# A thirteenth row buffer for three score-matrix pieces, half-block turns for all tiles, and a new order, in a fused spectral filter and expert lookup

## The chip, the cores and the metric

The kernel runs on one core of a Trainium2 chip. The metric is the device time of one execution in microseconds (us). The core has TensorE (PE in the profile, its weight loads PEld), VectorE (DVE), ScalarE (ACT), GpSimd (POOL), SyncE (SP) and 16 DMA engines. On-chip memory has 128 partitions; SBUF holds tiles, PSUM takes what TensorE writes.

## The reference

For `x` of 2048 tokens by 576 features the result is a gated sum of two branches.

```python
g = sigmoid((x * gate_w).sum(-1))
X = rfft2(x); a = irfft2(X * (w_r + 1j * w_i))          # branch A
q = einsum("nd,dhc->nhc", x, w_q)                        # branch B, 32 heads, 2 x 128 each
s1 = q[..., :128] @ k1.T;  s2 = q[..., 128:] @ k2.T      # 64 scores each
e  = argmax(s1) * 64 + argmax(s2)                        # one of 4096 experts a token and head
act = gelu(einsum("nd,nhd->nh", x, u[e]))
b = einsum("nh,nhd->nd", act, v[e])
out = g * a + (1 - g) * b
```

The softmax over one candidate is one in value. `u` and `v` are 4096 by 576 in float32, so a token needs 32 rows of `u` and 32 of `v`, which differ from token to token.

## The kernel before

**Tiles and chunks.** The tokens lie in 16 tiles of 128, the heads in 8 chunks of 4. Tiles 0 to 10 (`E_T`, "early") have their expert rows loaded while the scores are still being computed; tiles 11 to 15 (`L_SEQ`, "late") have theirs loaded in the second stage.

**First stage.** For each chunk the score weights and keys are multiplied into a score matrix in five pieces along the features. A piece is built by `build_m`: its weights are loaded by SyncE into a row buffer (`load_wq`, L428), TensorE multiplies them by the keys into half a PSUM buffer, ScalarE copies a rounded high piece to SBUF (`mh`, L526), TensorE subtracts that, and ScalarE copies the rest, the low piece (`ml`, L536). `MB` and `MBL` are the numbers of buffers for high and low pieces. `BUILD` says in which of the eight steps of a chunk each of the next chunk's pieces is built; two pieces of the same step share a PSUM buffer. A step (`scores`) multiplies two tiles of x, split in high and low parts as well, by the five pieces: 28 matmuls of 512 columns into one PSUM buffer. VectorE takes the maxima (L577), ScalarE marks them by signs (L584, L606), VectorE turns the marks into expert numbers (L608 to L626). `SOLO` counts first steps of chunk 0 that are read out one tile at a time.

**Row groups** (`group`). One group is a tile and a chunk: four gathers by GpSimd (L671), each bringing for 128 tokens the row of `u` and of `v` of one head, 4608 bytes a token, into one row buffer. The row buffers are the ring `uv` (`NG` of them), which the weight pieces share; the second stage has `NG2` more (`uv2`). VectorE multiplies the `u` rows by x and sums (L683), ScalarE applies the gelu (L689), VectorE multiplies in the factor (L698). Then there are two ways to sum the `v` rows, by the tile:

- way "v": VectorE adds each scaled row to the tile's sum (L711).
- way "t" (tiles in `T_T`): ScalarE scales each row into the other half of a neighbour's buffer (L724), and TensorE turns the scaled rows by an identity into PSUM, where they add up. For an early tile the PSUM sum of one group is added to the tile's sum by VectorE (L771); for a late one it grows over all chunks. `HALF` and `HALF_L` (early, late) choose between turns of 128x128 and two turns of 64x64 on half the partitions each (`turn`). `TJ` and `TJ_L` (early, late) say how many rows are scaled before a batch of turns is put out: a batch of two rows is one pair.

**Second stage.** It does the two-dimensional transform of branch A: fold the tiles (`fold`; tiles in `FOLD_V` are folded by VectorE first and need half as many matmuls), ten units of frequency work, the inverse per tile (`invert`; tiles in `INV_P` leave a sum and a difference to TensorE), the gates, the mix and the output. The late tiles' row groups run beside it in the order of `SEQ`, at which the last group of the late tile before the last is summed in way "v".

**The order.** All work is described as jobs with an engine, an estimated time, a due time and buffers. The class `Plan` simulates the engines with the ring sizes, always takes the ready job with the earliest due time whose buffers are free, and so writes one order for each engine. TensorE, VectorE, ScalarE, GpSimd and SyncE then run their lists strictly in that order, with waits where data or buffers are needed. Due times come from constants: `TP0` and `TPS` are the distance of score steps in chunk 0 and after it, `X0` and `X_GAP` place the loads of x, `LE` and `AHEAD` the row groups and their gathers, `TLAG` and `TGS` the late groups, `FPACE` the transform, the `AT_` constants single kinds of jobs. `LEAD`, `LEAST`, `LAND`, `ALONE`, `SHARE`, `DENSE` and `SLOWER` are the planner's model of gathers and of the TensorE clock.

Of the kernel before, what the change touches and what calls it, by code (L numbers as in the profile page):

```python
# [27 lines left out]
NCH = 8  # L28
# [60 lines left out]

LAG = {"DVE": 0.1, "ACT": 0.2, "PE": 0.0}  # L90
HOPS = {('PE', 'DVE'): 0.12, ('PE', 'ACT'): 0.46, ('PE', 'POOL'): 0.64, ('ACT', 'PE'): 0.28, ('ACT', 'DVE'): 0.02, ('ACT', 'POOL'): 0.01, ('DVE', 'POOL'): 0.4}
LEAD = 1.341
LEAST = -11.809
LAND = 4.039
ALONE = 0.716
SHARE = 0.426
WINDOW = 3.41
DENSE = -2.439
SLOWER = 1.649


class Plan:
# [37 lines left out]
    def order(self):  # L140
# [34 lines left out]
        def flow(t):  # L175
            nonlocal moved, turn
            both = bool(lines["POOL"] and lines["SP"])
            for e, q in lines.items():
                if q:
                    j = q[0]  # L180
                    rate = (1.0 if len(q) > 1 else ALONE) * (SHARE if both else 1.0) if e == "POOL" else (1.0 - SHARE if both else 1.0)
                    rest[j] = rest[j][0] - (t - moved) * rest[j][1], rate
# [9 lines left out]
        def clock(t, us, dense):  # L192
            nonlocal slow, window, seen
            x = t
            while True:
                k = int(x // WINDOW)
                if k != window:
                    slow = k > window + 1 or seen < DENSE * WINDOW
                    window, seen = k, 0.0
                edge = (k + 1) * WINDOW  # L200
                f = SLOWER if slow else 1.0
                if x + us * f <= edge:
# [15 lines left out]
        while events:  # L218
            t = events[0][0]
            while events and events[0][0] <= t:  # L220
# [8 lines left out]
                elif kind == "moved":  # L229
                    j, k = j  # L230
                    if k == turn:
                        flow(t)
                        lines[j.eng].popleft()
                        flow(t)
                        close(j, max(t, j.start + LEAST) + LAND if j.eng == "POOL" else t + 1.3)
                elif kind == "end":
# [10 lines left out]
            for eng, q in todo.items():  # L247
# [35 lines left out]
                if got.move:  # L283
                    push(t + (LEAD if eng == "POOL" else 1.9), "queue", got)
                else:
# [22 lines left out]
def tile_kernel(ctx, tc, xn, xT, wqT, wqL, kT, wri, uv, uw, gw, t_kr, t_fi, t_fe, t_tw, t_io, out):  # L308
# [32 lines left out]
    for tag, n in (("cand", CN), ("z", 8), ("b", 8), ("a", 8), ("im", 1), ("fe", 2), *((("dg", NDG),) if NDG else ()), ("mx", 2), ("sg", 2), ("sq", 1), ("ramp", 1), ("eq", EQN), ("sr", SRN)):  # L341
        ring(tag, "sm", n)
    ring("uv", "gp", NG)
    NY = len([t for t in T_T if t < NE])
# [115 lines left out]
    last = {}  # L460
# [200 lines left out]
    def group(t, c, at, ahead, gate_by=()):  # L661
# [49 lines left out]
                    dv(0.731, at, lambda v=v, s=s: stt(y.ap, v(), s(), y.ap, op0=ALU.mult, op1=ALU.add), [y], [(rows[k], 1), (a, k)])  # L711
            return
        part = t in E_T
        last = c == NCH - 1 - (TAILV if t == SEQ[-2][0] and t in T_T else 0)
        part_ = part and not paired(t, c)
        first = c == 0 or (part and not paired(t, c - 1))
        if first:
# [87 lines left out]
    order = sorted(((t, c) for c in range(NCH) for t in E_T), key=place)  # L805
    due = lambda n: when(n * 8 / NE + LE)
    todo = list(enumerate(order))
    for s in range(NCH * 8):
        c, tp = divmod(s, 8)
# [311 lines left out]

    TR = T0 + TLAG
    for n, t in enumerate(range(NT)):
# [44 lines left out]

NT2 = 5
SCRATCH = 2048  # L1170
NG = 12
NG2 = 3
LE = 3.125
NE = 11
MB = 8
MBL = 8
TPS = 7.047
AHEAD = -45.811
TLAG = 27.448
FPACE = 1.413  # L1180
BUILD = (3, 5, 6, 7, 7)
E_T = tuple(range(NE))
L_SEQ = tuple(range(NE, NT))
_PAIRS = ((14,), (13,), (12,), (11, 15))
SEQ = [(t, c) for p in _PAIRS for c in range(NCH) for t in p]
TGS = 8.225


LOW_PE = True
# [2 lines left out]
TRANS = 0.109  # L1192
TRANS2 = 0.062
SWITCH = 0.14
HALF = 0
HALF_L = 1
GX = 4
GT = 4
LOW_V = ()
LOW0 = 1  # L1200
LATE_G = 1
Z0 = 0.5
X0 = 9.48
TJ = 2
TJ_L = 4
BUILT = 0.1
ISSUE = 0.845
MOVE = 1.368
X_GAP = 4.311
GATE = -10.202  # L1210
HOLD_ML = 1.992
HOLD_A = 0.08
HOLD_T = 0.263
HOLD_D = 0.0
D_T = ()
T_T = (2, 3, 4, 6, 7, 10, 11, 12, 13, 14)
D_L = ()
FLIP = ()
AT_GELU = -46.223
AT_SCALE = 9.213  # L1220
AT_SUM = -94.03
AT_FOLD = -9.381
FOLD_V = (0, 1, 4, 5, 6, 8, 10, 11, 12, 13, 14)
GATE0 = 34.612
NA = 8
XL0 = -187.592
FI0 = -71.365
TURN = 1
MXO = 15.524
SGO = -56.575  # L1230
FILL = 0
FILLED = 8.11
TAILV = 1
TP0 = 12.235
X2 = 59.927
X4 = -0.154
XN0 = 11.008
INV_P = (0, 1, 2, 4, 8, 9, 10, 12, 14, 15)
SOLO = 0
SOLO_AT = -7.687  # L1240
SGO0 = 22.859
SOLO_P = 222.219
GL0 = 208.398
GL = 1.201
TWO = ()
CN = 3
EQN = 6
SRN = 4
ODD = (2, 7)


def paired(t, c):
    return t in TWO and c >= 0 and c + 1 < NCH and c % 2 == (t in ODD)


def how(t, c):
    if t == SEQ[-2][0] and c >= NCH - TAILV:
        return "v"
    if t in T_T:
        return "t"  # L1260
    return "d" if t in D_L or (t in D_T) != ((t, c) in FLIP) else "v"
# [49 lines left out]
```

## Time and profile before

| what | value |
|---|---|
| runs shown | 948.02, 948.95, 943.16 us, median 948.02 |
| profiled execution | 941.52 us, its span 939.7 us |
| instructions in the span | 18504 |
| moved by DMA | 344.16 MB, of them 302.02 MB by the gathers |
| row gathers | 512, first at 32.5 us, last at 918.5 us |

A group row of the profile reads: line, engine, operation, what it writes and reads, count, busy time, mean length of one in ns, idle time of the engine just before, and what ended that. A row of the order of time reads: start, length, engine, line, operation, tiles, shape, count, and in brackets the idle time before it with its releaser. A row of waits reads: who waited, for whom, us in total, times, longest. A row of a stretch reads: from and to, length, then busy time and instructions of each engine, the granted TensorE clock, the share of the DMA engines and the GB/s.

### The profile page before, as it was taken

The numbers are of one execution on the slowest core, as the hardware profiler recorded it, in microseconds if no ns is written. First come the engines' busy times: TensorE is split into PE (matmuls) and PEld (weight loads), VectorE is DVE, ScalarE is ACT, GpSimd is POOL, SyncE is SP. The second block draws the span as 40 slices with busy tenths as digits, with TensorE's granted clock in tenths as the row PEclk, the third lists the DMA queues.
The fourth block names the chain that finished last, engine by engine and source line by source line (L and its number), as shares of the span: only waits on it lengthen the run. The fifth ranks groups of instructions, "written<-read, shape, count | busy, mean of one in ns | idle before, by whom it ended". The sixth has DMA issues, their size and how long they took to land. (4 is left out here: it accounts for less than half of the span.)

```text
span 939.7 us, 18504 instructions
## 1 busy us (share of the span) xinstructions
PE 866.9 (92%) x6309; PEld 699.4 (74%) x6309; DVE 815.9 (87%) x2036; ACT 641.3 (68%) x2022; POOL 559.1 (59%) x516
## 2 busy tenths in 40 slices
PE   7899999999999998999999999967989999979993
PEld 6678887887877887888787777755767788756662
DVE  3578998998999999899999989898988898887888
ACT  3779888877877776876877777664646656654443
POOL 0416767756756656665665665667666556667560
PEclk9999999999999999999999999997999999999997
DMA  8968999999999999999999999899999999999993
GB/s 272 380 224 314 386 404 363 397 401 372 365 393 368 384 391 361 360 390 380 362 400 386 383 391 417 317 337 415 328 417 341 367 380 395 415 351 412 379 419 131
DMA packets 93218, 344.16 MB, mean 366 GB/s; under 512 B 10306, under 2 KB 14020, under 8 KB 93124
## 3 DMA queue, kind: packets, MB, share of 16 engines
q0 software_dynamic: 73728, 302.02, 83.7%
q1 hardware_dynamic: 19396, 40.96, 11.9%
q8 instruction: 50, 0.82, 0.3%
q14 instruction: 44, 0.36, 0.1%
HBM read 338.22 MB, written 4.72 MB: 365 GB/s over the span
## 5 line engine op out<-in xcount | busy, mean ns | idle before, releaser
L584 ACT ACTIVATE sg<-p,mx 128x64 bf16<-128x64 f32 x1024 | 227.1, 353 | 86.8 <-DVE mx L577 63.3
L671 POOL DMA_INDIRECT uv<-uv,eq x176 | 189.5, 1077 | 161.8 <-DVE xn L711 48.1
L683 DVE SCALAR_TENSOR_TENSOR uv<-uv,xn 128x576 f32<-128x576 f32 x352 | 259.9, 749 | 13.9 <-DMA uv<-uv,ei 4.6
L671 POOL DMA_INDIRECT uv<-uv,ei x178 | 199.9, 1123 | 104.8 <-issue 32.5
L724 ACT ACTIVATE uv<-uv,a 128x576 f32<-128x576 f32 x316 | 223.3, 784 | 19.7 <-DVE a L698 16.2
L372 PE MATMUL p<-ident,uv 64*128 64x64 f32 (+1 forms) x1980 | 159.7, 249 | 13.8 <-ACT uv L724 9.6
L372 PEld LDWEIGHTS p<-ident,uv 64*128 64x128 f32 (+1 forms) x1980 | 138.7, 140 | 41.3 <-ACT uv L724 16.7
L711 DVE SCALAR_TENSOR_TENSOR xn<-uv,a,xn 128x576 f32<-128x576 f32 x190 | 154.2, 812 | 0.5
L671 POOL DMA_INDIRECT uv<-uw,eq x80 | 88.2, 1103 | 52.5 <-issue 13.6
L683 DVE SCALAR_TENSOR_TENSOR uv<-uv,xl 128x576 f32<-128x576 f32 x160 | 116.0, 751 | 0.2
L372 PE MATMUL p<-mh,xha 128*128 128x512 f32 x256 | 106.3, 415 | 3.6 <-issue 2.4
L671 POOL DMA_INDIRECT uv<-uw,ei x78 | 81.2, 1042 | 41.0 <-issue 15.3
L372 PE MATMUL p<-mh,xh 128*128 128x512 f32 x256 | 103.5, 404 | 0.4 <-ACT sg L584 0.4
L372 PE MATMUL p<-ml,xha 128*128 128x512 f32 x256 | 101.1, 395 | 1.4 <-issue 1.4
L372 PE MATMUL p<-ml,xh 128*128 128x512 f32 x256 | 101.2, 395 | 0.6 <-issue 0.6
L372 PE MATMUL p<-mh,xoa 128*128 128x512 f32 x256 | 101.0, 395 | 0.5 <-issue 0.3
L372 PE MATMUL p<-mh,xo 128*128 128x512 f32 x256 | 101.1, 395 | 0.0
L372 PE MATMUL p<-fi,bt 128*128 128x289 f32 (+1 forms) x384 | 89.9, 429 | 1.1 <-ACT bt L917 0.7
L577 DVE TENSOR_REDUCE mx<-p 128x16 f32<-128x1024 f32 x64 | 77.9, 1218 | 13.9 <-PE p L372 11.8
L372 PEld LDWEIGHTS p<-fi,bt 128*128 128x128 f32 (+1 forms) x384 | 67.6, 242 | 19.1 <-issue 12.1
L606 ACT ACTIVATE sg<-sg 128x256 bf16<-128x256 bf16 x192 | 73.6, 424 | 0.8
L689 ACT ACTIVATE b<-z 128x4 f32<-128x4 f32 (+1 forms) x131 | 29.8, 228 | 62.7 <-DVE uv L683 52.1
(142 smaller groups left out, 1333.4 us busy)
## 6 DMA issues: line engine op xcount, KB each, us to landing
uv<-wqT SPq DMA_DIRECT2D x32, 512.0 KB
w<-wri SPq DMA_DIRECT2D x16, 289.0 KB
ml<-xT SPq DMA_DIRECT2D x16, 256.0 KB
xn<-xn SPq DMA_DIRECT2D x11, 288.0 KB
out<-xn SPq DMA_DIRECT2D x10, 288.0 KB
uv<-uv,ei POOLq DMA_INDIRECT x178
uv<-uv,eq POOLq DMA_INDIRECT x176
uv<-wqL SPq DMA_DIRECT2D x8, 256.0 KB
```

Source lines behind the costliest of these rows:

```text
L372: after("PE", nc.tensor.matmul(*args, **kw))
L577: dv(dve(1024), at - MXO, lambda: nc.vector.tensor_reduce(mv.ap[:, 2 * tp : 2 * tp + 2, :], ps.ap.rearrange("p a (g e) -> p a g e", e=E), ...
L584: on("ACT", actv(sg.ap[:, j, g, :], ps.ap[:, j, g * E : g * E + E], AF.Sign, bias=mv.ap[:, 2 * tp + j, g : g + 1], scale=-1.0))
L606: ac(0.307 if j is None else 0.2, at_, lambda b=b, s2=s2: actv(s2()[:, :, b * Q : b * Q + Q], s2()[:, :, b * Q : b * Q + Q], AF.Copy, bias ...
L671: on("POOL", nc.gpsimd.indirect_dma_start(out=g.ap.rearrange("p a d -> p (a d)"), out_offset=None, in_=table, in_offset=bass.IndirectOffse ...
L683: dv(0.677, at, lambda k=k, g=rows[k]: stt(g.ap[:, 0, :], g.ap[:, 0, :], 1.0, x.ap, op0=ALU.mult, op1=ALU.mult, accum_out=z.ap[:, k : k + 1]),
L689: ac(0.1, at + AT_GELU, lambda k0=k0, k1=k1: actv(b.ap[:, k0:k1], z.ap[:, k0:k1], AF.Gelu_apprx_tanh), [(b, k0)], [(z, k) for k in ks], ta ...
L711: dv(0.731, at, lambda v=v, s=s: stt(y.ap, v(), s(), y.ap, op0=ALU.mult, op1=ALU.add), [y], [(rows[k], 1), (a, k)])
L724: ac(0.667, at + AT_SCALE, lambda k=k, pair=pair, r=r: actv(pair.ap[:, r, :], rows[k].ap[:, 1, :], AF.Copy, scale=a.ap[:, k : k + 1]), [(p ...
```

## The change

The ring of row buffers has 13 in place of 12 in the first stage, and one fewer is added in the second, so that there are 15 as before. The high pieces have 7 buffers in place of 8, the low ones 6 in place of 8. Early tiles are turned in half blocks, as late ones are; their turns come in batches of four rows, those of the late tiles in batches of two. Tile 1 takes the place of tile 2 among those that are turned. Fewer tiles are folded by VectorE first (5, were 11), more are inverted without VectorE's sum and difference (12, were 10). Two steps of chunk 0 are read out one tile at a time. The late tiles come in the order 11, 12, 13, then 14 and 15 in turn. The due times and the planner's constants are new. The function `tail`, with `TAILW`, gives how many of a tile's last chunks are summed in way "v"; tile 15 is not in `T_T`, so that with these constants it is one chunk of tile 14, where it was one of tile 11.

```diff
--- before.py
+++ after.py
@@ -89,14 +89,14 @@
 
 LAG = {"DVE": 0.1, "ACT": 0.2, "PE": 0.0}
 HOPS = {('PE', 'DVE'): 0.12, ('PE', 'ACT'): 0.46, ('PE', 'POOL'): 0.64, ('ACT', 'PE'): 0.28, ('ACT', 'DVE'): 0.02, ('ACT', 'POOL'): 0.01, ('DVE', 'POOL'): 0.4}
-LEAD = 1.341
-LEAST = -11.809
-LAND = 4.039
-ALONE = 0.716
-SHARE = 0.426
+LEAD = 1.171
+LEAST = -32.411
+LAND = 3.551
+ALONE = 0.636
+SHARE = 0.3
 WINDOW = 3.41
-DENSE = -2.439
-SLOWER = 1.649
+DENSE = -3.314
+SLOWER = 1.108
 
 
 class Plan:
@@ -711,7 +711,7 @@
                     dv(0.731, at, lambda v=v, s=s: stt(y.ap, v(), s(), y.ap, op0=ALU.mult, op1=ALU.add), [y], [(rows[k], 1), (a, k)])
             return
         part = t in E_T
-        last = c == NCH - 1 - (TAILV if t == SEQ[-2][0] and t in T_T else 0)
+        last = c == NCH - 1 - tail(t)
         part_ = part and not paired(t, c)
         first = c == 0 or (part and not paired(t, c - 1))
         if first:
@@ -1168,22 +1168,22 @@
 
 NT2 = 5
 SCRATCH = 2048
-NG = 12
-NG2 = 3
-LE = 3.125
+NG = 13
+NG2 = 2
+LE = 2.716
 NE = 11
-MB = 8
-MBL = 8
-TPS = 7.047
-AHEAD = -45.811
-TLAG = 27.448
-FPACE = 1.413
-BUILD = (3, 5, 6, 7, 7)
+MB = 7
+MBL = 6
+TPS = 7.168
+AHEAD = -4.994
+TLAG = 93.11
+FPACE = 2.205
+BUILD = (2, 5, 5, 6, 6)
 E_T = tuple(range(NE))
 L_SEQ = tuple(range(NE, NT))
-_PAIRS = ((14,), (13,), (12,), (11, 15))
+_PAIRS = ((11,), (12,), (13,), (14, 15))
 SEQ = [(t, c) for p in _PAIRS for c in range(NCH) for t in p]
-TGS = 8.225
+TGS = 6.424
 
 
 LOW_PE = True
@@ -1192,69 +1192,76 @@
 TRANS = 0.109
 TRANS2 = 0.062
 SWITCH = 0.14
-HALF = 0
+HALF = 1
 HALF_L = 1
+TAILW = 1
 GX = 4
 GT = 4
 LOW_V = ()
 LOW0 = 1
 LATE_G = 1
 Z0 = 0.5
-X0 = 9.48
-TJ = 2
-TJ_L = 4
+X0 = 11.332
+TJ = 4
+TJ_L = 2
 BUILT = 0.1
-ISSUE = 0.845
-MOVE = 1.368
-X_GAP = 4.311
-GATE = -10.202
-HOLD_ML = 1.992
-HOLD_A = 0.08
-HOLD_T = 0.263
+ISSUE = 0.658
+MOVE = 1.325
+X_GAP = 5.028
+GATE = 5.201
+HOLD_ML = 1.359
+HOLD_A = 0.372
+HOLD_T = 0
 HOLD_D = 0.0
 D_T = ()
-T_T = (2, 3, 4, 6, 7, 10, 11, 12, 13, 14)
+T_T = (1, 3, 4, 6, 7, 10, 11, 12, 13, 14)
 D_L = ()
 FLIP = ()
-AT_GELU = -46.223
-AT_SCALE = 9.213
-AT_SUM = -94.03
-AT_FOLD = -9.381
-FOLD_V = (0, 1, 4, 5, 6, 8, 10, 11, 12, 13, 14)
-GATE0 = 34.612
+AT_GELU = 7.361
+AT_SCALE = 35.318
+AT_SUM = -22.122
+AT_FOLD = 6.917
+FOLD_V = (3, 4, 5, 13, 14)
+GATE0 = -38.732
 NA = 8
-XL0 = -187.592
-FI0 = -71.365
+XL0 = -138.691
+FI0 = 23.463
 TURN = 1
-MXO = 15.524
-SGO = -56.575
+MXO = 17.776
+SGO = -61.118
 FILL = 0
 FILLED = 8.11
 TAILV = 1
-TP0 = 12.235
-X2 = 59.927
-X4 = -0.154
-XN0 = 11.008
-INV_P = (0, 1, 2, 4, 8, 9, 10, 12, 14, 15)
-SOLO = 0
-SOLO_AT = -7.687
-SGO0 = 22.859
-SOLO_P = 222.219
-GL0 = 208.398
-GL = 1.201
+TP0 = 3.086
+X2 = 40.417
+X4 = -7.538
+XN0 = 102.218
+INV_P = (0, 1, 3, 4, 5, 6, 8, 9, 10, 11, 14, 15)
+SOLO = 2
+SOLO_AT = 28.542
+SGO0 = -15.951
+SOLO_P = 143.698
+GL0 = 251.794
+GL = 4.111
 TWO = ()
 CN = 3
 EQN = 6
 SRN = 4
-ODD = (2, 7)
+ODD = (1, 3, 4, 7)
 
 
 def paired(t, c):
     return t in TWO and c >= 0 and c + 1 < NCH and c % 2 == (t in ODD)
 
 
+def tail(t):
+    if t not in T_T:
+        return 0
+    return TAILW if t == SEQ[-1][0] else TAILV if t == SEQ[-2][0] else 0
+
+
 def how(t, c):
-    if t == SEQ[-2][0] and c >= NCH - TAILV:
+    if c >= NCH - tail(t):
         return "v"
     if t in T_T:
         return "t"
```

## The prediction

> **What bounds the kernel now.** I read the page first, then the stretches by stage, then what the row loads wait for, then TensorE in order of time. The page shows two resources near their end at once.
>
> ```profile
> span 939.7 us, 18504 instructions
> PE 866.9 (92%) x6309; PEld 699.4 (74%) x6309; DVE 815.9 (87%) x2036; ACT 641.3 (68%) x2022; POOL 559.1 (59%) x516
> ...
> DMA packets 93218, 344.16 MB, mean 366 GB/s; under 512 B 10306, under 2 KB 14020, under 8 KB 93124
> ```
>
> A whole-run share hides which stage is worth something, so the stretches come next. The cut at 75 us is about where chunk 0 of the scores ends, 575 is in the last chunk, and from 650 on there are only late tiles and the transform.
>
> ```profile
> core 0: us, PE busy (x) PEld busy (x) DVE busy (x) ACT busy (x) POOL busy (x), PEclk, DMA share, GB/s
> 75.00:575.00 500.00, 481.51 (x3234) 397.52 (x3233) 457.12 (x1139) 390.92 (x1366) 325.65 (x297) 0.99 0.99 381
> 575.00:650.00 75.00, 64.90 (x425) 54.01 (x423) 66.10 (x171) 51.33 (x172) 48.32 (x44) 0.93 0.95 361
> 650.00:925.00 275.00, 254.42 (x2129) 195.81 (x2130) 237.67 (x602) 148.57 (x306) 170.18 (x159) 0.97 0.98 379
> 925.00:940.00 15.00, 0.53 (x6) 0.39 (x4) 11.53 (x27) 2.13 (x8) 0.00 (x0) 0.62 0.12 49
> ...
> 350.00:375.00 25.00, 22.32 (x177) 17.74 (x177) 24.97 (x60) 16.32 (x63) 16.44 (x15) 0.94 0.99 366
> 475.00:500.00 25.00, 24.80 (x180) 20.45 (x180) 23.70 (x61) 20.47 (x74) 15.92 (x15) 1.00 1.02 405
> 550.00:575.00 25.00, 21.32 (x103) 17.24 (x102) 21.49 (x53) 16.79 (x62) 16.49 (x15) 0.93 1.03 418
> ```
>
> In the 500 us from 75 to 575 TensorE is busy 481.5 us (96%), VectorE 457.1 (91%), and the DMA engines show a share of 0.99. The last figure is less final than it looks: at the same share of about one they moved 366 GB/s in one stretch and 405 and 418 in two others. So packets can be in flight all the time and still be slow, and 381 GB/s is not the most that these loads reach. The stretch with 366 is one in which VectorE has no pause (24.97 of 25). What the loads wait for says why.
>
> ```profile
> POOL uv L671 <- issue: 55.7, 169, 1.1
> POOL uv L671 <- DVE xn L711: 38.8, 28, 2.6
> POOL uv L671 <- ACT uv L724: 29.7, 24, 4.2
> POOL uv L671 <- PE p L372: 16.2, 19, 3.6
> ```
>
> These are GpSimd's waits from 75 to 575. The 169 of the first row are the pause of about 0.3 us after each issue. The others are waits for a row buffer to come free: the row sum on VectorE (L711), the scaling on ScalarE (L724), the turn on TensorE (L372). The loop is closed: load a row, use it, free it, load the next. I read TensorE as the pacemaker of the score stage, with VectorE and the loads close behind.
>
> **The change part by part.** *Turns of the early tiles.* Six of the eleven early tiles have their rows turned on TensorE, in 8 chunks: 48 groups of two pairs, before and after. Before, a pair is 9 turns of 128x128; after, both pairs go in one batch of 36 turns of 64x64, the form that the late tiles have already.
>
> ```profile
> 305.57 1.14 PE L372 MATMUL p<-ident,uv 128*128 128x128 f32 x9
> 306.47 0.47 PE L372 MATMUL p<-mh,xha 128*128 128x512 f32 x1
> 306.78 0.39 PE L372 MATMUL p<-ml,xha 128*128 128x512 f32 x1
> 307.01 0.40 PE L372 MATMUL p<-mh,xoa 128*128 128x512 f32 x1
> ...
> 739.58 1.28 PE L372 MATMUL p<-ident,uv 64*128 64x64 f32 x36
> 740.78 2.56 PE L372 MATMUL p<-tw,t 128*128 128x256 f32 x16
> ...
> 749.36 1.13 PE L372 MATMUL p<-ident,uv 64*128 64x64 f32 x26
> ...
> 752.69 2.22 PE L372 MATMUL p<-t,tw 128*128 128x289 f32 x8
> ```
>
> Starts are what counts, since matmuls overlap. A pair in full blocks holds TensorE from 305.57 to 306.47, 0.90 us, so a group costs 1.80. A batch in half blocks holds it from 739.58 to 740.78, 1.20 us. Saved: 0.60 a group, 48 x 0.60 = 29 us of TensorE.
>
> ```profile
> 75.00:575.00 500.00, 97.58 (x738) 84.73 (x738) 0.00 (x0) 0.99 0.99 381
> ```
>
> This row is the turns alone from 75 to 575: 738 matmuls, 82 pairs, 41 groups; 41 x 0.60 = 25 us less in that stretch. Not all becomes time. With 25 us off, 475 would be left for VectorE's 457 (96%), and the loads would have to run at 381 x 500/475 = 401 GB/s, which the stretch at 475 shows to be possible but which is not the rule. I count three quarters, **-18 us**. The ends: 0 if the loop of row buffers, not TensorE, is what holds; -29 if it is TensorE alone.
>
> The Trainium skill speaks against this edit: "TensorEngine Tiling (Array Packing)", section "Key Properties", says that a change of tiling mode drains TensorE. The next matmul after the batch at 739.58 starts 1.20 us later, so an emptying is already in that figure or is small, and a pair in full blocks pays 0.08 as well (306.47 to 306.78 is 0.31, 306.78 to 307.01 is 0.23). By the rule the sum would lose a part of the 29 us that the page does not size.
>
> *The thirteenth row buffer* has no cost of its own: one more row can be on its way. By itself it is worth between 0 and what the loads lose (381 against 405 GB/s over 500 us, 30 us). I count it as what lets the loads keep up with the 18 us above, and nothing more: batches of two pairs also keep the first pair's rows until the fourth is scaled, which is two scalings (L724) longer, and so eats part of it. *The order of tiles* (row sums on VectorE for tiles 0, 2, 5, 8, 9 in place of 0, 1, 5, 8, 9) leaves the number of instructions as it was, but takes two of those groups apart where VectorE is full (350 to 375). It is in the same 18 us.
>
> *The opening.*
>
> ```profile
> 31.09 0.38 SPq L469 DMA_DIRECT2D mh<-xT  x1
> 46.86 0.33 SPq L428 DMA_DIRECT2D uv<-wqT  x1
> 47.28 1.33 SPq L473 DMA_DIRECT2D ml<-xT  x3
> ...
> 48.43 1.22 DVE L577 TENSOR_REDUCE mx<-p 128x16 f32<-128x1024 f32 x1 [6.24 <-PE p L372]
> ...
> 47.03 0.94 POOL L671 DMA_INDIRECT uv<-uw,eq  x1 [2.15 <-remote]
> 65.97 0.93 POOL L671 DMA_INDIRECT uv<-uv,eq  x1 [18.00 <-DVE xn L711]
> ```
>
> SyncE's queue stands from 31 to 47 on a weight piece of chunk 1 (L428), which lives in a row buffer and finds none free; three loads of x (L473) stand behind it, no scores can run, and VectorE is idle for 6.24 us. Then the row loads stand for 18 us, all buffers full. After, the pieces are due earlier (the first eight steps are 3.1 us apart, not 12.2), ahead of the gathers that fill the ring, tiles 0 to 3 are read out singly, which brings the first indices sooner, and there is one buffer more. The loads moved ahead (576 x 1024 float32 a chunk, 2.4 MB, some 6 us at 381 GB/s) then delay late x tiles. Ends: 0 to -12; I take most of the 6.24, **-5 us**.
>
> *Fewer pieces of the score matrix.* Five high and five low pieces serve a chunk. Before, three of each can be made ahead; after, two high and one low. The next chunk's pieces are built in steps 2, 5, 5, 6, 6 (before 3, 5, 6, 7, 7), so two PSUM buffers of the four wait half built for a low piece that comes free only in step 7, where pieces end one after another. Behind them on TensorE stand scores and turns, which need PSUM as well.
>
> ```profile
> PE p L372 <- ACT ml L536: 2.3, 3, 1.1
> PE p L372 <- ACT mh L526: 1.1, 1, 1.1
> ...
> L577 DVE TENSOR_REDUCE mx<-p 128x16 f32<-128x1024 f32 x64 | 77.9, 1218 | 13.9 <-PE p L372 11.8
> ...
> 32.16 2.54 ACT L584 ACTIVATE sg<-p,mx 128x64 bf16<-128x64 f32 x12
> ```
>
> Today the pieces cost TensorE 3.4 us in the whole stretch. The trace has no chunk with fewer pieces. Ends: 0 (the shorter turns hand PSUM back sooner), and a full readout uncovered in two steps of each of 7 seams: 1.22 for the maximum and 8 signs at 2.54/12 = 0.21 make 2.9 us, x 14 = 41 us. I take twice today's, **+3 us** more, near the lower end, because only the last steps of a chunk are hit.
>
> *Work moved to TensorE in the second stage.*
>
> ```profile
> L372 PE MATMUL p<-kr,f 128*128 128x128 f32 x88 | 15.4, 324 | 10.9 <-DVE f L891 10.9
> L372 PE MATMUL p<-kr,f 128*64 128x128 f32 x44 | 5.6, 339 | 0.0
> L372 PE MATMUL p<-kr,xn 128*128 128x128 f32 x64 | 8.1, 280 | 0.0
> L372 PE MATMUL p<-kr,xn 128*64 128x128 f32 x16 | 2.0, 294 | 0.5 <-issue 0.4
> L372 PE MATMUL p<-kr,xn 128*32 128x128 f32 x16 | 1.9, 284 | 0.8 <-issue 0.8
> L372 PE MATMUL p<-t,krb 128*128 128x289 f32 x104 | 28.8, 419 | 1.1 <-issue 0.6 <-ACT t L1083 0.4
> ```
>
> A folded tile takes 21.0/11 = 1.9 us of TensorE, an unfolded one 12.0/4 = 3.0; six tiles go over, +6.6 us, and VectorE is rid of twelve half-width sums and differences. They fall where TensorE has room (64.9 of 75 from 575 to 650), so I count **+1**; without that room it is 6.6. Two more inverse tiles without VectorE's sum and difference: 8 matmuls more at 28.8/104 = 0.28, 2.2 us, in a stretch with TensorE at 254 of 275: **+1** after what VectorE gains. The late tiles' batches are halved (31 groups, one more batch each): at the 0.08 seen at a change of form 2.5 us, less for rows freed sooner: **+2**. The transform falls due later against the late tiles; TensorE has work either way. I count 0, ends -5 and +12: 12 is what VectorE does alone in the last 15 us, were as much again left over. The new constants of the planner change nothing but order.
>
> Sum: -18 - 5 + 3 + 1 + 1 + 2 = **-16 us**. It is made against the profiled execution, 941.5 us around its span of 939.7; that one is the quickest of those shown, 6.5 below the median 948.0. The saving is taken off the median: **932 us**.
>
> **Rivals.** *The loads hold, not TensorE.* The share of 0.99 speaks for it, and rows freed late under batches of four; also batches torn by waits, as the one at 749.36: 26 turns at first, and 3.33 us until the next work at 752.69, which would save nothing. Then the turns' gain is idle time on TensorE, the seams' 3 us are hidden beside the loads, and -5 of the opening and +4 of the second stage are left: 947. Against it are 405 and 418 GB/s in the trace. The Trainium skill would side with this rival: "DMA: Bandwidth & Descriptors", section "Where 436 GB/s comes from", has HBM bind at about 358 GB/s a core; the stretches at 405 and 418 show that it does not hold for this core. *PSUM at the seams* (the slower side): the 41 us above in place of 3: 948 - 16 + 38 = 970. It turns the result from the point where a seam stalls by 16/7 = 2.3 us more than I count. Against it: turns in batches need PSUM for less time. *Everything opens up*: TensorE's 29, the opening's whole 12, no cost at the seams: 948 - 29 - 12 + 4 = 911; the 418 GB/s speak for it, VectorE's 91% against.
>
> **How the numbers follow.** Forecast 0.47, loads hold 0.23, everything opens up 0.17, PSUM 0.13. The range takes in the forecast's unknowns, the first rival's 947 with some spread and most of the way to 911: 913 to 951. About 1% (9.5 us) is what a measurement of this kernel can tell from no change. Under 938.5 lie 0.43 of the forecast's chance and all of 0.17: 0.60 faster. Within 1%: 0.04 and 0.23 and a little of PSUM, 0.28. Slower: 0.12.
>
> **What would show it.** Right: batches of 36 in the score stage that start the next matmul after 1.2 to 1.3 us; the last scores some 20 us sooner than now; over 390 GB/s from 75 to 575; GpSimd's 18 us wait gone. Wrong: TensorE idle before scores in the last steps of each chunk, released by ScalarE's low pieces (L536) or signs (L584); turns torn by waits for L724; a tail longer than 15 us with inverse tiles in it.

## The result, and the profile after

The kernel after takes **979.67 us** (median of 4 runs, 976.69 to 984.73); the kernel before took 948.49 beside it (4 runs, 943.16 to 951.68). The ratio is **1.033, with a 95% interval of 1.028 to 1.037**: slower. The forecast was 932 with a range of 913 to 951. The profiled execution after took 984.73 us, its span is 982.9; before, these were 941.52 and 939.7. The one after is the slowest of its four and the one before is quicker than all that are listed: their spans differ by 43 us, the medians by 31, so some 12 of the 43 lie in which executions were profiled.

The page of the kernel after, its first lines (busy time of each engine, and what DMA moved):

```profile
span 982.9 us, 20425 instructions
...
PE 870.9 (89%) x7253; PEld 682.3 (69%) x7253; DVE 807.5 (82%) x2034; ACT 644.2 (66%) x2024; POOL 556.9 (57%) x516
...
DMA packets 93225, 344.27 MB, mean 350 GB/s; under 512 B 10306, under 2 KB 14020, under 8 KB 93124
```

The bytes are nearly the same and VectorE is busy a little less long, but 43 us of span were added. The stretches tell where. First after, then the one stretch of before that was not shown yet, in the columns of the prediction's stretches:

```profile
25.00:75.00 50.00, 39.39 (x176) 28.95 (x174) 28.93 (x76) 31.72 (x128) 13.42 (x14) 0.90 0.74 267
75.00:575.00 500.00, 455.67 (x3930) 363.47 (x3931) 429.44 (x1082) 374.41 (x1303) 302.49 (x278) 0.97 0.95 356
575.00:650.00 75.00, 68.11 (x512) 54.97 (x511) 63.80 (x165) 58.22 (x220) 40.52 (x38) 0.95 0.93 352
650.00:925.00 275.00, 242.32 (x2141) 187.04 (x2140) 228.86 (x591) 146.48 (x305) 177.68 (x165) 0.94 0.98 371
```

```profile
25.00:75.00 50.00, 45.90 (x318) 35.55 (x317) 34.27 (x84) 38.02 (x149) 14.78 (x15) 0.93 0.82 297
```

Every engine does less in the opening, and every engine does less in the 500 us of the score stage: TensorE 456 in place of 482, VectorE 429 in place of 457, the loads 356 GB/s in place of 381. By these figures nothing has become full. The trace's 512 row loads serve as mile posts: the first starts at 32.8 us (32.5 before), the first load of chunk 1's groups (the 45th) at 132.4 (121.1), the last one of the early tiles at 684.2 (646.3), the end is 298.7 us behind that (293.5). So **the opening costs 11 us, the rest of the score stage 27, the second stage 5**. From the 45th load to the last early one the pace is 79.1 us for 44 loads, one chunk, after and 75.3 before. This pace is used below for other runs too.

The turns alone, from 75 to 575, as the prediction showed them of before:

```profile
75.00:575.00 500.00, 55.31 (x1368) 47.34 (x1368) 0.00 (x0) 0.97 0.95 356
```

TensorE is busy with turns for 55.3 us in place of 97.6, in 38 batches. Busy times overlap; what counts is starts:

```profile
306.26 1.33 PE L372 MATMUL p<-ident,uv 64*128 64x64 f32 x36
307.51 0.50 PE L372 MATMUL p<-mh,xq 128*128 128x512 f32 x1
307.85 0.40 PE L372 MATMUL p<-ml,xq 128*128 128x512 f32 x1
```

A batch takes 1.25 us here (306.26 to 307.51), and the two changes of form, worked out below under e13, bring it to 1.45. A group in full blocks takes 2 x 0.98 = 1.96. So about 0.51 us a group is saved by the records, 19 us in the 38 batches. That much of the step happened. What became of it is seen in TensorE's waits from 75 to 575 (who waited for whom, us in total, times, longest), after and then before:

```profile
PE p L372 <- DVE yt L771: 16.3, 5, 4.8
PE p L372 <- issue: 13.6, 30, 1.4
PE p L372 <- ACT ml L536: 4.7, 6, 2.6
PE p L372 <- ACT yt L769: 3.2, 1, 3.2
```

```profile
PE p L372 <- issue: 7.5, 19, 0.6
PE p L372 <- ACT uv L724: 6.7, 8, 2.2
```

The wait for L771 is new. L771 is VectorE adding a group's turned sum to the tile's sum, which frees the PSUM buffer. One such wait in order of time, on TensorE, then the copies of the pieces on ScalarE and the sum on VectorE, all after:

```profile
534.22 2.08 PE L372 MATMUL p<-kT,uv 128*64 128x64 f32 x64
...
542.80 1.33 PE L372 MATMUL p<-ident,uv 64*128 64x64 f32 x36
548.44 0.79 PE L372 MATMUL p<-mh,xh 128*128 128x512 f32 x1 [4.31 <-DVE yt L771]
549.03 0.63 PE L372 MATMUL p<-ml,xh 128*128 128x512 f32 x1
549.46 0.63 PE L372 MATMUL p<-mh,xo 128*128 128x512 f32 x1
```

```profile
526.36 0.60 ACT L526 ACTIVATE mh<-p 128x512 fp32r<-128x512 f32 x1 [2.04 <-PE p L372]
...
550.98 0.60 ACT L536 ACTIVATE ml<-p 128x512 fp32r<-128x512 f32 x1 [5.08 <-PE p L372]
...
553.96 0.60 ACT L526 ACTIVATE mh<-p 128x512 fp32r<-128x512 f32 x1 [1.89 <-PE p L372]
...
559.11 0.63 ACT L536 ACTIVATE ml<-p 128x512 fp32r<-128x512 f32 x1
```

```profile
547.56 0.82 DVE L771 TENSOR_TENSOR yt<-p,yt 128x640 f32<-128x640 f32 x1 [1.54 <-remote]
```

A piece whose high part was copied at 526.36 has its low part copied at 550.98, 24.6 us later. The two pieces multiplied at 534.22 have their high parts copied only at 553.96 and later, the last low part at 559.11, since no piece buffer is free. Two of the four PSUM buffers are held that long; the scores and the group's sum share the other two, and the next score step must wait until L771 has read the sum. The trace has a second part to this wait: L771 itself starts 3.4 us after the last turn's record ends (547.56 against 544.13), and for the last 1.54 of them VectorE is idle until a release that the profile can't name ("remote"). VectorE's waits for turned sums from 75 to 575, after, then before:

```profile
DVE yt L771 <- remote: 21.1, 8, 3.5
DVE yt L771 <- PE p L372: 12.7, 12, 3.4
```

```profile
DVE yt L771 <- PE p L372: 9.6, 9, 2.0
DVE yt L771 <- remote: 7.2, 7, 1.8
```

In all four stalls listed below L771 starts 2.0 to 3.9 us after the end of the last turn's record. Whether the turns really end later than their records or only the sign of their end comes late, the trace doesn't tell; in the first case a part of TensorE's idle time here is work. The last pieces of that chunk in the kernel before, TensorE and then ScalarE:

```profile
516.76 2.03 PE L372 MATMUL p<-kT,uv 128*64 128x64 f32 x53
```

```profile
523.18 0.60 ACT L526 ACTIVATE mh<-p 128x512 fp32r<-128x512 f32 x1 [0.58 <-PE p L372]
524.46 0.62 ACT L526 ACTIVATE mh<-p 128x512 fp32r<-128x512 f32 x1
526.86 0.58 ACT L536 ACTIVATE ml<-p 128x512 fp32r<-128x512 f32 x1
528.04 0.60 ACT L536 ACTIVATE ml<-p 128x512 fp32r<-128x512 f32 x1 [0.50 <-PE p L372]
```

There everything is through at 528.64, 11.9 us after the first key matmul. Over all pieces built from chunk 1 on, the time from the first key matmul to the end of the low copy is 10.0 us a piece before and 23.1 after, on the average. The stall comes back chunk by chunk: in four of them, 9 to 11 us ahead of the chunk's last score, a score step starts late, at 311.55, 388.07, 467.58 and 548.44, after waits of 3.29, 2.88, 4.76 and 4.31 us for L771. Behind it the score matmuls start 0.43 us apart (549.03, 549.46) in place of 0.23: the granted clock is 0.5 from 547.0 to 553.8. In all it is 0.5 for 34.1 us from 75 to 600 after, for 6.8 before.

The opening. Here are the loads of x, with the start of the first and the last, before and then after, and SyncE's longest waits up to 95 us after:

```profile
L473 SPq DMA_DIRECT2D ml<-xT x16: 309/358/503, 2.1 to 48.3; - x16
```

```profile
L473 SPq DMA_DIRECT2D ml<-xT x16: 327/328/737, 2.1 to 73.8; - x16
```

```profile
SPq L473 <- DVE xoa L477: 13.6, 2, 11.9
SPq L428 <- DVE uv L683: 13.0, 1, 13.0
SPq L473 <- DVE xo L477: 10.1, 5, 3.0
```

The last tile of x is loaded 25.5 us later, and SyncE waits for VectorE to have split an earlier tile (L477). The reason stands in `split_x`: x is loaded into a buffer of the pieces, `y = buf(("ml", "mh"), ...)`, and split from there. In chunk 0 the five pieces of each kind occupy ten of them; of 16 buffers six are left for x, of 13 only three. The rows and the code fit this; e15 and e16 below test it.

### The profile page after: what moved, and what is told of

It is laid out like the page before. It is cut to its first block, busy times and chain, and to the rows that moved or that the text cites. A ratio compares the mean times of both kernels' runs of the same rounds, so it can differ in the third digit from the quotient of the medians.

```text
span 982.9 us, 20425 instructions
## 1 busy us (share of the span) xinstructions
PE 870.9 (89%) x7253; PEld 682.3 (69%) x7253; DVE 807.5 (82%) x2034; ACT 644.2 (66%) x2024; POOL 556.9 (57%) x516
## 4 chain that ended last, share of the span: by engine, by line
PE 47%; DVE 21%; ACT 10%; another core or an unknown queue 5%; issue 5%; DMA 5%; POOL 2%; POOLq 0%; DVEq 0%; ACTq 0%; SPq 0%
PE p L372 47%; DVE uv L683 8%; DVE xn L711 4%; ACT sg L584 4%; ACT uv L724 3%; DMA uv<-uv,ei 2%; POOL uv L671 2%; DVE mx L577 1%; DMA uv<-uv,eq 1%; DVE yt L771 1%; DMA uv<-uw,ei 1%; ACT sg L606 1%; ACT ml L536 1%; ACT mh L526 1%
## 5 line engine op out<-in xcount | busy, mean ns | idle before, releaser
L671 POOL DMA_INDIRECT uv<-uv,ei x178 | 194.0, 1090 | 104.3 <-issue 30.9
L584 ACT ACTIVATE sg<-p,mx 128x64 bf16<-128x64 f32 x1024 | 230.0, 375 | 32.2 <-DVE mx L577 15.7
L724 ACT ACTIVATE uv<-uv,a 128x576 f32<-128x576 f32 x316 | 224.7, 780 | 27.8 <-DVE a L698 18.8
L372 PEld LDWEIGHTS p<-ident,uv 64*128 64x128 f32 x2844 | 103.9, 140 | 61.8 <-issue 34.3
L372 PE MATMUL p<-ident,uv 64*128 64x64 f32 x2844 | 122.0, 229 | 27.7 <-issue 15.2
L372 PE MATMUL p<-mh,xh 128*128 128x512 f32 x256 | 109.3, 427 | 21.8 <-DVE yt L771 18.6
L671 POOL DMA_INDIRECT uv<-uw,ei x78 | 84.9, 1088 | 56.7 <-ACT uv L724 18.3
L372 PE MATMUL p<-ml,xh 128*128 128x512 f32 x256 | 105.3, 411 | 0.0
L372 PE MATMUL p<-mh,xo 128*128 128x512 f32 x256 | 105.3, 411 | 0.0
L372 PE MATMUL p<-fi,bt 128*128 128x289 f32 (+1 forms) x384 | 93.2, 438 | 1.9 <-issue 1.4
L372 PEld LDWEIGHTS p<-fi,bt 128*128 128x128 f32 (+1 forms) x384 | 68.6, 243 | 21.2 <-issue 11.9
L606 ACT ACTIVATE sg<-sg 128x256 bf16<-128x256 bf16 (+1 forms) x198 | 78.8, 455 | 0.8
```

What stands on the lines that cost most here:

```text
L372: after("PE", nc.tensor.matmul(*args, **kw))
L584: on("ACT", actv(sg.ap[:, j, g, :], ps.ap[:, j, g * E : g * E + E], AF.Sign, bias=mv.ap[:, 2 * tp + j, g : g + 1], scale=-1.0))
L606: ac(0.307 if j is None else 0.2, at_, lambda b=b, s2=s2: actv(s2()[:, :, b * Q : b * Q + Q], s2()[:, :, b * Q : b * Q + Q], AF.Copy, bias ...
L671: on("POOL", nc.gpsimd.indirect_dma_start(out=g.ap.rearrange("p a d -> p (a d)"), out_offset=None, in_=table, in_offset=bass.IndirectOffse ...
L724: ac(0.667, at + AT_SCALE, lambda k=k, pair=pair, r=r: actv(pair.ap[:, r, :], rows[k].ap[:, 1, :], AF.Copy, scale=a.ap[:, k : k + 1]), [(p ...
```

## The experiments

The kernel before took 948 us beside the kernel after, and beside the runs below 960 (chip 0: e1 to e4), 894 and 891 (chip 5: e5 to e8, e9 to e12), 949 (chip 1: e13 to e16) and 893 (chip 4: e17, e18). So only ratios to the kernel before beside it are compared, with 95% intervals; paces are compared between runs in which the kernel before was about as fast. The kernel after itself was not run on the quick chips, 4 and 5, and no changed kernel ran on two chips: that a ratio carries over from one chip to another is taken for granted and not shown. The traces differ, too: waits of VectorE before the turned sum that end in "remote" are in every trace of chips 0 and 1, in that of before and in that of after, and in none of the ten of chips 4 and 5. A change of a constant also changes the order that the planner writes, except where the text says that the order was kept.

**The half-block turns**

e1: the turns of the after kernel in the kernel before.

```diff
-HALF = 0
+HALF = 1
-TJ = 2
+TJ = 4
```

> The kernel before with one part of the change alone: early tiles turned in half blocks, in batches of four rows (HALF 1, TJ 4). If TensorE's time sets the pace of the score stage and a batch really costs 1.2 us in place of 1.8, 15 to 20 us less: about 930. If row buffers and PSUM set it, and a batch of four rows holds both longer, no change or up to 10 us more: 945 to 960.

Measured: 1.010 (1.006 to 1.014). Half blocks alone lose.

e5: half blocks, but in pairs as before.

```diff
-HALF = 0
+HALF = 1
```

> The kernel before with half-block turns of the early tiles, batches of one pair as before (HALF 1, TJ 2 unchanged). If the batches of four rows are what made the half blocks alone 1.0% slower, this is 1 to 2% faster than before (ratio 0.98 to 0.99). If the half blocks end late for whoever waits for their sum, 1.00 to 1.02 again.

Measured: 1.020 (1.015 to 1.025). Batches of four show no more harm than pairs, though on another chip. Both kernels have an order of their own, which e13 and e14 take away.

e13: the order of the kernel before on every engine, kept by leaving the planner's cost as it was; only the turns go out as half blocks in pairs.

```diff
-plan("PE", 9 * len(pairs) * TRANS2 + SWITCH if half else ...
+plan("PE", 9 * len(pairs) * TRANS2 + SWITCH if half and t >= NE else ...
-HALF = 0
+HALF = 1
```

> The kernel before with the early tiles turned in half blocks, but the planner still told the time of full blocks: every engine's list is that of before, only the turns themselves are other instructions. If TensorE's time sets the pace, 2 to 3% faster (ratio 0.97 to 0.98). If row buffers and loads set it, 0.995 to 1.005: the 25 us become pauses on TensorE. If half blocks as such do harm (a late end, the clock), 1.01 to 1.02, as with the new plan.

e14: the reverse, the order of e5 with full blocks; the planner is given the half-block cost for all.

```diff
-plan("PE", 9 * len(pairs) * TRANS2 + SWITCH if half else ...
+plan("PE", 9 * len(pairs) * TRANS2 + SWITCH, ...
```

> The opposite: full blocks as before, but the planner told the time of half blocks, so every list is that of the half-block kernel that ran at 1.020. If the order is what costs there, 1.02 or more; if the half blocks cost, 1.00.

Measured: e13 1.012 (1.008 to 1.017), e14 1.003 (1.001 to 1.006). In one and the same order half blocks in pairs cost 1.2% (e13), and 1.020/1.003 = 1.7% in the other (e5 against e14, which ran on different chips). With half blocks in pairs, then, the order is not the cause; the turns are. TensorE in order of time in e13:

```profile
316.93 0.39 PE L372 MATMUL p<-ml,xha 128*128 128x512 f32 x1
317.16 0.39 PE L372 MATMUL p<-mh,xoa 128*128 128x512 f32 x1
317.48 0.78 PE L372 MATMUL p<-ident,uv 64*128 64x64 f32 x18
318.19 0.50 PE L372 MATMUL p<-mh,xha 128*128 128x512 f32 x1
318.53 0.40 PE L372 MATMUL p<-ml,xha 128*128 128x512 f32 x1
318.76 0.39 PE L372 MATMUL p<-mh,xoa 128*128 128x512 f32 x1
```

Scores start 0.23 us apart (316.93 to 317.16), but the first turn comes 0.32 after a score (317.16 to 317.48) and the second score 0.34 after the first (318.19 to 318.53). A change of form costs 0.09 on the way in and 0.11 on the way out, so a pair of 18 takes 0.71 + 0.20 = 0.91 beside a full pair's 0.90 + 0.08 = 0.98 of the prediction's rows: 0.07 us is saved. The Trainium skill, "TensorEngine Tiling (Array Packing)", section "Key Properties", has a change of tiling mode drain TensorE; these rows agree and give the size. And the stretch and the waits of e13:

```profile
75.00:575.00 500.00, 469.49 (x3933) 366.56 (x3930) 447.46 (x1113) 383.56 (x1337) 308.77 (x288) 0.98 0.98 369
```

```profile
PE p L372 <- ACT uv L724: 14.7, 21, 1.9
PE p L372 <- issue: 11.4, 30, 1.1
```

TensorE does less, not more: 469 in place of 482 of 500. It waits for the scaled rows (L724) 14.7 us in place of 6.7, and the clock is at 0.5 for 27.3 us from 75 to 600 in place of 6.8. At half the rate, 20.5 us more cost some 10, the waits (with "issue") 12 more; less 82 x 0.07 = 6 saved, that is an estimate of +16, and the last early load is 18 us later than before (664.3 against 646.3); by the medians e13 lost 13 us (961.3 against 948.6). On the quick chip the clock goes the same way: it is at 0.5 for 31.5 us from 75 to 600 in e5 and for 3.4 in e8, a kernel with full blocks. VectorE's waits for the turned sums (L771) grow as well, from 16.8 us before to 33.0 in e13. That waits and clock are the cause is argued by these sums; the slowdown itself is shown.

**Row buffers and pieces**

e7: one row buffer fewer in the first stage.

```diff
-NG = 12
-NG2 = 3
+NG = 11
+NG2 = 4
```

> The kernel before with one row buffer fewer in the first stage (NG 11, NG2 4, so 15 in the second as before). The price of a row buffer from the other side: if row buffers set the pace, ratio 1.02 to 1.04; if TensorE sets it, 1.00 to 1.01.

Measured: 1.042 (1.039 to 1.046). The pace of a chunk is 76.2 us, against 72.9 in e8 on a chip as fast. Row buffers do set the pace, on the side of fewer.

e2: the trade of the change in the kernel before, with the old `BUILD`; e6: the missing pieces alone.

```diff
-NG = 12          # e2 only
-NG2 = 3          # e2 only
+NG = 13          # e2 only
+NG2 = 2          # e2 only
-MB = 8
-MBL = 8
+MB = 7
+MBL = 6
```

> The kernel before with the trade of buffers alone (NG 13, NG2 2, MB 7, MBL 6; steps of the builds as before). If the thirteenth row buffer is worth something by itself, 935 to 943. If the missing pieces cost PSUM at the seams, 955 to 975, with TensorE waiting before the first scores of steps 6 and 7. If neither, 948 within 5.

> The kernel before with 7 high and 6 low pieces but the row ring left at 12 (MB 7, MBL 6). If the missing pieces alone cost the 12% of the whole trade, ratio 1.10 to 1.14. If the thirteenth row buffer or its planning has a part in it, under 1.08.

Measured: e2 1.123 (1.116 to 1.130), e6 1.062 (1.058 to 1.066). Fewer pieces with the old building steps are far worse than what the change made of them. A piece is in PSUM for 30.5 us in e2 and 20.7 in e6 (10.0 before). That e2, with one row buffer more, loses twice as much as e6 (on another chip) is not explained.

e9: the trade of e2 with the new building steps as well.

```diff
-BUILD = (3, 5, 6, 7, 7)
+BUILD = (2, 5, 5, 6, 6)
```

> The kernel before with the trade of buffers (NG 13, NG2 2, MB 7, MBL 6) and the new steps of the builds (2, 5, 5, 6, 6). With the old steps the trade cost 12%. If pairs that wait half built in PSUM are the harm, the early steps make it worse or leave it: 1.11 to 1.16. If the harm is that pieces come too late for the next chunk, the early steps mend most of it: 1.02 to 1.06.

Measured: 1.027 (1.023 to 1.032), so the earlier building mends most of it. What is left lies in the opening: the 45th load starts at 129.2 us (113.9 in e8), with this on TensorE in chunk 0:

```profile
63.40 0.39 PE L372 MATMUL p<-ml,xq 128*128 128x512 f32 x1
72.92 0.80 PE L372 MATMUL p<-mh,xh 128*128 128x512 f32 x1 [9.13 <-ACT sg L584]
```

From there the pace is 72.3 us a chunk, against 72.9: **the thirteenth row buffer and the missing pieces together moved the pace by 0.6 us a chunk.** What each of them did alone, e9 can't tell. A piece is in PSUM for 22.5 us here, nearly as long as in the kernel after (23.1), and TensorE waits 5.8 us for the group sum from 95 to 600: pieces held this long do not by themselves slow the score stage on this chip.

e18: a thirteenth row buffer whose room comes from an early tile, with all pieces kept.

```diff
-NE = 11
+NE = 10
-NG = 12
-NG2 = 3
+NG = 13
+NG2 = 2
-_PAIRS = ((14,), (13,), (12,), (11, 15))
+_PAIRS = ((14,), (13,), (12,), (10,), (11, 15))
```

> The kernel before with 13 row buffers whose room comes from an early tile in place of the score pieces: 10 early tiles, tile 10 moved to the late ones (its groups between those of tile 12 and those of 11 and 15), 13 buffers in the first stage and 2 more in the second, 8 and 8 pieces. The first stage has 40 gathers a chunk in place of 44, the second 32 more. If row buffers alone set the first stage's pace (a buffer held for 19.7 us, a chunk then 40 x 19.7 / 13 = 61 us), it is up to 100 us shorter there and some 55 us longer in the second stage: ratio about 0.95. If TensorE's work is the floor of a chunk there (of 72 us a chunk it is busy 96%, and one turned tile less saves about 2 us of it), the first stage gains 15 to 30 us and the second loses 55: 1.03 to 1.045. If the data rate alone set both stages, the loads only move from one to the other: 0.99 to 1.01.

Measured: 1.030 (1.028 to 1.032). The stretch of e18, and below it that of e17 from the same chip (12 buffers, 11 early tiles):

```profile
75.00:575.00 500.00, 493.88 (x3354) 409.76 (x3353) 461.55 (x1144) 399.21 (x1439) 310.40 (x285) 1.00 0.96 372
```

```profile
75.00:575.00 500.00, 494.89 (x3384) 412.69 (x3383) 478.55 (x1191) 406.95 (x1448) 342.36 (x307) 1.00 1.01 398
```

TensorE is at 99% in both. With 40 groups' loads a chunk and 13 buffers the pace is 68.8 us, against 71.3: the 2.5 us are near the turns that one tile fewer takes off TensorE (two pairs, 1.96 us), and far from the 61 us a chunk that the row buffers alone would give. I read this so: on a quick chip TensorE is a floor just below the pace that twelve buffers give; eleven lie above it (e7), and a thirteenth has little left to win.

**The opening**

e15: e9 with x staged in free row buffers too; e16: the kernel after with the same edit.

```diff
-        y = buf(("ml", "mh"), [P, 4, P])
+        y = buf(("ml", "mh", "uv"), [P, 4, P])
```

> The trade of buffers with early builds in the kernel before (it ran at 1.027, with chunk 0 ending 20 us late), but x may be staged in a free row buffer too when no piece buffer is free. If the opening is late because x is staged in the buffers of the pieces, of which three are gone, chunk 0 ends 10 to 20 us sooner and the ratio is 1.00 to 1.015. If it is late for another reason, 1.02 to 1.03 again.

> The changed kernel with the same staging of x in free row buffers. If the opening costs it the 11 us that the first 44 gathers lag behind, 1.015 to 1.025 in place of 1.033; if not, 1.03 to 1.04.

Measured: e15 1.013 (1.008 to 1.017), half of e9's loss, though on another chip; its 45th load starts 4.8 us later than in e14 on the same chip (127.1 against 122.3), where e9's was 15.3 later than e8's. e16 1.034 (1.028 to 1.039), no gain. The opening is mended in e16; here are its loads of x and its stretch:

```profile
L476 SPq DMA_DIRECT2D ml<-xT x16: 327/430/972, 2.1 to 24.4; - x16
```

```profile
25.00:75.00 50.00, 45.98 (x332) 36.32 (x331) 39.73 (x107) 41.38 (x159) 19.63 (x19) 1.00 0.88 321
```

The 45th load starts at 123.0 in place of 132.4. But the pace is still 78.5 us a chunk, the waits for the group sum (L774 there) are 23.0 us in 10 from 95 to 600, and the end is 304 us behind the last early load in place of 299. So the staging is shown as the cause of most of the late opening, and by the ratios of e9 and e15 it is about half of what the trade costs in the kernel before; that it costs the kernel after anything in the end is not shown.

e4: the kernel after with the old due times of the opening.

```diff
-TP0 = 3.086
-X0 = 11.332
+TP0 = 12.235
+X0 = 9.48
...
```

(and so on for `X_GAP`, `X2`, `X4`, `XN0`, `SOLO`, `SOLO_AT`, `SGO0`, `SOLO_P`)

> The changed kernel with the old due times of the opening (TP0, X0, X_GAP, X2, X4, XN0 and the single readout of the first tiles, SOLO 0). Chunk 0 ended 12 us later after the change than before; if the new opening is the cause and the rest of the kernel cannot make it up, 965 to 970. If the row loads later absorb it, within 5 of 980.

Measured: 1.057 (1.050 to 1.065). The new due times are not what is wrong; without them the kernel is slower still (its 45th load starts at 131.2 us, and 52 us lie behind its last load).

**Parts undone in the kernel after**

The four edits, in the order e3, e10, e11, e12:

```diff
-BUILD = (2, 5, 5, 6, 6)
+BUILD = (3, 5, 6, 7, 7)
```

```diff
-NG, NG2, MB, MBL = 13, 2, 7, 6
+NG, NG2, MB, MBL = 12, 3, 8, 8
```

```diff
-HALF = 1
+HALF = 0
```

```diff
-TJ = 4
+TJ = 2
```

> The changed kernel with the old steps for the builds alone (BUILD 3, 5, 6, 7, 7 in place of 2, 5, 5, 6, 6). If pairs of pieces that wait half built hold two PSUM buffers through steps 5 to 7, this gives back most of TensorE's 24 us of waits for the row sums' eviction (L771): about 960. If the waits come from the batches of four or from the number of pieces and not from the early steps, within 5 of 980.

> The changed kernel with the old buffers (NG 12, NG2 3, MB 8, MBL 8), all else as after. If the trade is a net loss in the changed kernel too, 1.00 to 1.02 of before in place of 1.033. If the thirteenth row buffer pays for the missing pieces there, 1.04 to 1.08: one row buffer fewer cost 4.2% in the kernel before.

> The changed kernel with the early tiles turned in full blocks (HALF 0, batches of four rows kept). TensorE has 25 us more to do in the score stage. If the pace there is TensorE's, 1.05 to 1.06; if half blocks cost by holding rows and PSUM longer, 1.01 to 1.03.

> The changed kernel with batches of one pair for the early tiles (TJ 2). If batches of four rows keep row buffers and set the pace by that, 1.00 to 1.02; if single batches cost TensorE more than they free, 1.035 to 1.05.

Measured: e3 1.068 (1.060 to 1.076), e10 1.045 (1.039 to 1.051), e11 1.042 (1.037 to 1.047), e12 1.044 (1.040 to 1.048). No single undoing brings the ratio under the 1.033 of the kernel after, with the caution that e3 ran on chip 0 and the others on chip 5, where the kernel after was not run. For e11 and e12 the trace shows where time is lost, and it is not in the turns of the score stage. The end of e11:

```profile
870.00:900.00 30.00, 30.00 (x175) 21.64 (x175) 22.90 (x53) 13.14 (x29) 6.11 (x6) 1.00 0.66 268
900.00:930.00 30.00, 17.90 (x75) 11.71 (x74) 9.21 (x13) 6.59 (x14) 0.00 (x0) 0.88 0.15 60
```

The last row load starts 49 us ahead of the end (27 in the kernel after, 21 before): the new order leaves inverse work behind the loads. In the score stage, though, e11 and e12 run at 72.2 and 72.5 us a chunk, e10, with batches of four half blocks and all pieces, at 76.1, e8 at 72.9, all on chips as fast. TensorE's waits for the group sum from 95 to 600 go with it: 6.3 us in e11, 7.6 in e12, 5.8 in e9, 0.9 in e8, but 11.9 in e10 and 23.0 in e16. So on the quick chip the slower pace goes with batches of four half blocks and not with the missing pieces: e9, e11 and e12 have as few pieces and run no slower than e8. The 23.0 us of e16 are from chip 1 and can't be set beside the others: 20.3 us of VectorE's waits for the sum end in "remote" there from 95 to 600, none in e10. This is a pattern and not a proof: the orders differ, and e1, with batches of four and all pieces, lost no more than e5 with pairs (on another chip) and waited 5.6 us for the group sum (75 to 575).

**What costs nothing**

e8: only the planner's model of after in the kernel before (`LEAST`, `LAND`, `ALONE`, `DENSE`, `SLOWER` too).

```diff
-LEAD = 1.341
-SHARE = 0.426
+LEAD = 1.171
+SHARE = 0.3
...
```

e17: only the second stage's part (`FOLD_V`, `INV_P`, `FPACE`, `TLAG`, `TGS`, `AT_FOLD` too).

```diff
-_PAIRS = ((14,), (13,), (12,), (11, 15))
-TJ_L = 4
+_PAIRS = ((11,), (12,), (13,), (14, 15))
+TJ_L = 2
...
```

> The kernel before with the planner's model of gathers and clock from after (LEAD, LEAST, LAND, ALONE, SHARE, DENSE, SLOWER), which change no work, no buffer and no due time, only the order that the planner writes. If the order is as good with either, ratio 0.995 to 1.005, as the prediction held. If the constants of a kernel belong together, 1.01 to 1.05: a part of what the single edits cost is then the order and not the edit.

> Only the second stage's part of the change, put into the kernel before: the late tiles in the order 11, 12, 13, then 14 and 15 in turn, their turns in batches of two, the fold and inverse lists and FPACE, TLAG, TGS, AT_FOLD of the kernel after; ring, pieces, early turns and opening as before. My forecast priced this part at +4 us (late batches +2, folds +1, inverse +1): ratio 1.004, the time behind the last early gather longer by some 4 us, and nothing different ahead of it. Rival, that the part missing from my account sits in the second stage (there the kernel after is 5.2 us longer): 1.005 to 1.015, the tail longer by 5 to 13 us. Rival, that the second stage is set by the gathers alone and hides all this: 1.000.

Measured: e8 1.004 (1.002 to 1.007), e17 1.0004 (0.998 to 1.003). Neither carries the loss.

## Why the prediction was wrong, point by point

**TensorE as the pacemaker: half right.** e18 and e17 show it at 99% on a quick chip, and e7 shows that one row buffer fewer costs 4.2%. Both limits lie within a few per cent of one another. The failed step is the inference: that time taken off TensorE would come off the stage, three quarters of it. By the records the freed time became waits, TensorE busy 456 of 500, and the score stage got 27 us longer.

**Early turns in half blocks, -18: the sign was wrong.** e13 and e5 against e14 put half blocks in pairs at +1.2% and +1.7%, e1 batches of four at +1.0% with a new order. The price on TensorE was nearly right: "an emptying is already in that figure or is small" is half true, for the figure ran from the first turn to the next matmul and both changes of form lie outside it, but in a batch of four they make 0.51 us a group of the forecast's 0.60. In pairs they leave only 0.07 us a pair. What failed is the step from there to the stage: the 19 us that the records show as saved from 75 to 575 were not turned into time.

**Thirteenth row buffer, 0 of its own: not contradicted** in the score stage: with the missing pieces it moved the pace by 0.6 us (e9, 72.3 against 72.9). The trade was not free, which stands under the next two.

**Opening, -5: measured +11.** I followed the queue and the wait for a row buffer (L428), and did not ask what else lives in the buffers that are taken away. The rows that I quoted say it: `ml<-xT`, x is loaded into a low piece's buffer. Of six buffers left beside chunk 0's ten pieces, three were gone. e16 brings the loads of x forward again, the last of them from 73.8 to 24.4 us.

**Fewer pieces at the seams, +3: the waits came where it put them, and it mis-sized them.** I had described two PSUM buffers half built for a low piece that comes free in step 7, and priced it at twice a wait of 3.4 us, since the trace of before shows no more. A wait that is small with three spare pieces says nothing about one spare. Measured: a piece holds PSUM 23.1 us in place of 10.0, and the waits on L771 and L769 are 19.5 us from 75 to 575, with four more spells at half clock up to 600. That the held pieces cause all of it is not shown: e9 holds them as long and keeps its pace, and a part of these waits is the late "remote" release before L771.

**Folds +1, inverse +1, late batches +2, transform 0:** e17 measures 1.0004, so together nothing that can be told from zero.

**"The new constants of the planner change nothing but order":** by itself 0.4% (e8). But e3, e4, e11 and e12, with one constant put back (ten in e4), stand at 1.042 to 1.068, on other chips, where the kernel after stands at 1.033. The reading is that an order fits one set of sizes; e11 shows what another order can cost: 49 us behind the last load in place of 27.

**The rivals.** "PSUM at the seams" (0.13, 970) came nearest. I had it turn the result from 2.3 us more a seam; four of the seams stall for 2.9 to 4.8. It named the wrong releaser (signs and maxima, L584; it was the group sum, L771) and lacked the half clock behind. "The loads hold" would have left TensorE's gain idle and the total at 947; idle it was by the records, but the loads ran at 356 GB/s, while e17 moved 398 over the same stretch. Of what the prediction named as signs of an error, "TensorE idle before scores in the last steps of each chunk" is what came.

**How the loss adds up.** e9 (the trade, 1.027) and e13 or e1 (half blocks, 1.010 to 1.012) multiply to 1.037 to 1.039, a little more than the 1.033 of the whole; with re-planned orders and different chips no better agreement can be asked. Open is how the 27 us of the score stage divide between batches of four, held PSUM and the late release before L771, what that release is, and why e16's mended opening brings nothing.

## What to carry to other kernels

Before a buffer is taken from a pool, list every kind of data that passes through that pool in every stage, the first one above all: a part of the cost turned up where x is staged, not where the pieces are used. Do not price a scarcer resource by the waits that the trace shows while it is plentiful; ask how long each buffer would be held, and what shares the PSUM that it holds meanwhile. And time taken off a busy engine pays only if what feeds it and drains it can follow: a batch that is shorter but arrives in other portions can leave the engine idle, and at a lower clock besides.

## What the runs showed of the hardware

- **The clock falls even in a kernel with TensorE at over 90%.** In and after the pause of 4.31 us that ended at 548.44 the granted clock was 0.5 from 547.0 to 553.8, 6.8 us. The Trainium skill, "TensorE: Matmul & The Clock Gate", section "Why this matters for your kernels", warns of pauses above about 3 us; these rows agree. But shorter ones can go with it: in e13 no wait of TensorE's from 75 to 575 is listed with more than 1.9 us, and from 75 to 600 the clock was at 0.5 for 27.3 us all the same. In that stretch there were six spells after (34.1 us) and two before (6.8).
- **A change of form on TensorE** took 0.09 us on the way into 64x64 turns (0.32 from start to start in place of 0.23) and 0.11 on the way out (0.34).
- **The same kernel differs by 7% between chips and occasions**, 891 to 960 us for the kernel before. On the slower ones VectorE's waits for TensorE's turned sums end late, in a release that the profile can't name ("remote": 21.1 us in 8 after, 7.2 in 7 before, from 75 to 575); on the quicker ones no such wait is listed. What lies behind it is open.
